# Feature products of an LSH-masked attention: all 64 rows of a head's block instead of 13

## The chip, the cores and the metric

The kernel runs on one core of one Trainium2 chip. Its metric is the device time of one execution in microseconds (us). A core has TensorE (PE; its weight loads are listed as PEld), VectorE (DVE), ScalarE (ACT), GpSimd (POOL), SyncE (SP, which here issues DMAs) and DMA engines. Each engine runs its own list of instructions in order and waits for the others through semaphores. All matmuls write PSUM, which has 128 partitions and 8 banks of 512 float32 values per partition.

## The reference

Four batches of eight heads, 768 positions, 64 values a head. The attention looks only at keys in the same hash bucket as the query; the bucket is the sign pattern of six projections. A gMLP follows.

```
q_bits = (einsum('bhsd,dk->bhsk', q, proj) > 0);  k_bits likewise
mask   = q_bucket[:, :, :, None] == k_bucket[:, :, None, :]      # bucket = the 6 bits as a number
scores = where(mask, q @ k^T / sqrt(64), -1e9)
scores = scores - max(scores);  attn = exp(scores)
attn   = attn / (sum(attn) + 1e-9)
x      = (attn @ v), heads side by side                          # 4 x 768 x 512
...
h = gelu(x @ w_in);  u, v = halves of h;  v_n = layernorm(v) * g_ln
out = x + (u * (w_sg @ v_n + b_sg)) @ w_out
```

## The kernel before, in words

Attention works on 16 head pairs (4 batches, 4 pairs of heads). The two heads of a pair lie one above the other on the 128 partitions: head j has partitions 64j to 64j+63. Every score matmul is issued twice, once a head, with 64 or fewer rows starting at partition 0 or 64, and each writes its own PSUM bank.

For each pair `load` fetches q, k and v; `parts` transposes q and k and splits them into a high and a low half (`hq`, `lq`, `hk`, `lk`: two float32r numbers that together carry the float32 value); `features` (L496, L499) projects them with `pwh`/`pwl` and turns the signs into feature tiles `fq` and `fk`. A feature tile has 128 partitions, in two blocks of 64, one a head (`BL` = 64). In a block row 0 is for the shift of the softmax, rows 1 to 12 hold two signs for each of the six bits, and rows 13 to 63 are zero, because the projection matrix has zero columns there and the threshold and factor of those rows are zero. The product of a query's and a key's feature columns is 0 where all bits agree and at most -2^33 where one differs, so that adding it to the score is the mask.

`largest` (called maxima below) takes a tile of 128 queries. For each half of the keys (384) it adds two products in one bank a head: features first, then `hq` with `hk` (L517). A DVE reduction over each bank (L524) gives the largest score. `shift` turns three tiles' maxima into row 0 of the query features (L533, L539, L545). `weigh` then computes, for half of the queries (384) and tiles of 128 keys, the transposed scores: `hk` with `hq`, `lk` with `hq`, `hk` with `lq`, and the features last, which now also subtract the largest score (L562); ACT takes the exponential into `p` (L568); one call does two key tiles and ends with the product with `v` (L574, eight matmuls with float32 operands); POOL and DVE add up the rows (L583). `finish` divides (L599 to L621) and stores x to DRAM.

The order on each engine is not that of the source. Every step is entered with `plan.add`, with an engine, an estimated cost, a priority, and what it reads and writes. `Plan.order` makes a list schedule out of these and `run` issues the instructions in that order. A maxima group of one key half is entered with a PE cost of 0.36 us, a weigh group of one key tile with 0.71, the value products of two key tiles with 1.48; a cost of 0.09 is added where a group's form differs from that of the group ahead ("row" for maxima and weigh, "col" for value products). Maxima run five query tiles ahead of their use (`AHEAD`). Score tiles take any of seven PSUM banks that is free (`ps_tile`), the value product has the eighth. The splitting of the gMLP's input weights (L352 to L361, mostly DVE) is spread over the first pairs. After attention the pools are released and the gMLP runs, batch by batch (L766, L795, L813, L839).

The change touches `block`, which gives the 13 rows of a head's block, `largest` and `weigh`.

## Time and profile before

| what | us |
|---|---|
| median of 3 runs | 949.92 (948.51 to 952.18) |
| profiled execution, its own time | 944.45 |
| its span, first to last instruction | 942.7 |
| TensorE busy | 916.1 |
| VectorE busy | 620.5 |
| ScalarE busy | 419.5 |
| GpSimd busy | 316.7 |
| granted TensorE clock, mean over the span | 0.971 of full speed |

Attention lasts until about 592 us, the gMLP from there to the end. In a group of the profile, "13*128 13x384" means a matmul with 13 rows (the contraction) and 128 columns that streams 384 elements; x384 is the count of instructions; then come busy time in us, the mean duration of one in ns, and the idle time of the engine ahead of them with what ended it. In the timeline a row gives start and duration in us, and joins neighbours of one kind. A matmul's end is modelled, and neighbours overlap, so the distance of two starts says what a step costs, not the duration.

### The profile page before, as it was taken

How to read it: one execution, taken by the hardware profiler on the slowest of the kernel's cores; microseconds unless marked ns; L12 is line 12 of the kernel's file. 1: busy time of each engine (PE TensorE's matmuls, PEld its weight loads, DVE VectorE, ACT ScalarE, POOL GpSimd, SP SyncE). 2: the span in 40 equal slices, each digit the busy share in tenths (PEclk: the TensorE clock that was granted, in tenths of full speed). 3: DMA queues.
4: the chain of work that ended last, by engine and by line, in shares of the span. 5: the costliest groups of instructions: out<-in, count | busy, mean ns of one | idle time of the engine just before them, and what ended most of it. 6: DMA issues, size and time to landing. Idle time of an engine off the chain costs nothing.

```text
span 942.7 us, 15438 instructions
## 1 busy us (share of the span) xinstructions
PE 916.1 (97%) x5480; PEld 615.7 (65%) x5480; DVE 620.5 (66%) x1369; ACT 419.5 (45%) x926; POOL 316.7 (34%) x342
## 2 busy tenths in 40 slices
PE   7999999999999999999999999887989999999998
PEld 5655555554555555555555555576978998998996
DVE  7777787887778765665565653598996425732930
ACT  2445545544555445454444447355243414522511
POOL 0334444443434344244242426513420320340120
PEclk8999999998999999999998999998999999999999
DMA  5121331331321221221202102342002322103003
GB/s 128 40 79 38 81 87 40 87 88 40 88 65 53 77 51 44 73 55 44 68 27 67 43 19 77 96 153 90 29 23 79 107 85 77 34 17 119 1 1 112
DMA packets 100589, 60.85 MB, mean 65 GB/s; under 512 B 65696, under 2 KB 92320, under 8 KB 100512
## 3 DMA queue, kind: packets, MB, share of 16 engines
q1 hardware_dynamic: 99200, 56.85, 21.2%
q10 hardware_dynamic: 1312, 3.02, 1.0%
q8 instruction: 43, 0.70, 0.3%
q14 instruction: 34, 0.28, 0.1%
HBM read 47.06 MB, written 12.68 MB: 63 GB/s over the span
## 4 chain that ended last, share of the span: by engine, by line
PE 83%; DVE 9%; DMA 4%; issue 1%; SPq 1%; ACT 1%; POOL 0%; ACTq 0%; DVEq 0%
PE g L562 21%; PE av L574 15%; PE g L517 14%; PE ps_vs L813 8%; PE ps_o L839 7%; PE ps_h L795 5%; PE ps_h L766 4%; PE g L496 3%; PE g L474 3%; PE g L539 2%; PE g L599 1%; DMA rs<-r 1%; PE ps_o L844 1%; DMA q<-in_q_dram 1%; DVE owx L353 1%
## 5 line engine op out<-in xcount | busy, mean ns | idle before, releaser
L524 DVE TENSOR_REDUCE mx<-g 128x1 f32<-128x384 f32 x384 | 192.0, 548 | 132.4 <-PE g L517 132.2
L568 ACT ACTIVATE p<-g 128x384 f32<-128x384 f32 x384 | 168.1, 487 | 221.4 <-PE g L562 217.6
L583 POOL TENSOR_TENSOR sum<-sum,p 128x384 f32<-128x384 f32 x128 | 126.9, 1017 | 193.8 <-ACT p L568 180.8
L574 PE MATMUL av<-p,v 128*64 128x385 f32 x768 | 154.9, 527 | 0.0
L517 PE MATMUL g<-hk,hq 64*128 64x384 f32 x384 | 86.2, 445 | 0.0
L574 PEld LDWEIGHTS av<-p,v 128*64 128x64 f32 x768 | 48.5, 141 | 56.0 <-issue 52.4
L562 PE MATMUL g<-fq,fk 13*128 13x384 f32 x384 | 84.5, 436 | 0.0
L562 PE MATMUL g<-hq,hk 64*128 64x384 f32 x384 | 83.6, 431 | 0.0
L583 DVE TENSOR_TENSOR sum<-sum,p 128x384 f32<-128x384 f32 x128 | 68.8, 561 | 19.8 <-ACT p L568 15.5
L517 PE MATMUL g<-fk,fq 13*128 13x384 f32 x384 | 81.3, 417 | 0.0
L562 PEld LDWEIGHTS g<-hq,hk 64*128 64x128 f32 x384 | 36.7, 187 | 64.7 <-issue 49.4
L583 POOL TENSOR_TENSOR sum<-p,p 128x384 f32<-128x384 f32 x64 | 64.0, 1019 | 36.4 <-ACT p L568 35.8
L751 DVE SCALAR_TENSOR_TENSOR h<-h,ps_h 128x384 f32<-128x384 f32 (+1 forms) x56 | 33.2, 605 | 62.8 <-ACT h L750 62.5
L562 PEld LDWEIGHTS g<-fq,fk 13*128 13x128 f32 x384 | 35.4, 181 | 48.6 <-issue 48.6
L562 PE MATMUL g<-hq,lk 64*128 64x384 f32 x384 | 66.1, 339 | 0.0
L562 PE MATMUL g<-lq,hk 64*128 64x384 f32 x384 | 65.6, 336 | 0.0
L839 PE MATMUL ps_o<-woh,gs 128*128 128x512 f32 x192 | 65.5, 402 | 0.0
L813 PE MATMUL ps_vs<-wgh,zh 128*128 128x384 f32 x192 | 64.3, 335 | 0.1
L813 PE MATMUL ps_vs<-wgh,zl 128*128 128x384 f32 x192 | 64.3, 335 | 0.0
L813 PE MATMUL ps_vs<-wgl,zh 128*128 128x384 f32 x192 | 64.2, 334 | 0.0
L517 PEld LDWEIGHTS g<-hk,hq 64*128 64x128 f32 x384 | 36.3, 186 | 39.5 <-issue 39.5
L621 POOL TENSOR_TENSOR xt<-xt,e 128x384 f32<-128x384 f32 x32 | 32.2, 1005 | 83.1 <-ACT e L619 78.4
(127 smaller groups left out, 1679.9 us busy)
## 6 DMA issues: line engine op xcount, KB each, us to landing
q<-in_q_dram SPq DMA_DIRECT2D x32, 192.0 KB, 3.2
k<-in_k_dram SPq DMA_DIRECT2D x32, 192.0 KB, 3.5
v<-in_v_dram SPq DMA_DIRECT2D x16, 384.0 KB, 4.1
rs<-r SPq DMA_DIRECT2D x64, 96.0 KB, 2.9
xs<-xt SPq DMA_DIRECT2D x32, 192.0 KB, 1.8
x<-xs SPq DMA_DIRECT2D x16, 384.0 KB, 3.3
rx<-xs SPq DMA_DIRECT2D x96, 64.0 KB, 2.0
out_dram<-ob SPq DMA_DIRECT2D x24, 256.0 KB, 2.1
```

The source lines that it names most:

```text
L517: nc.tensor.matmul(sc[kh][j]()[:, :SH], x[0]()[r, qs], x[1]()[r, kh * SH:(kh + 1) * SH], start=(n == 0), stop=(n == 1))
L524: plan.add(DVE, 0.56, prio, lambda j=j, kh=kh: nc.vector.tensor_reduce(mx()[:, kh, i, j:j + 1], sc[kh][j]()[:, :SH], axis=AX.X, op=ALU.max ...
L562: nc.tensor.matmul(sc[i][j]()[:, :SH], x()[r, ks], y()[r, cs], start=(n == 0), stop=(n == 3))
L568: plan.add(ACT, 0.5, prio, lambda i=i, j=j: nc.scalar.activation(p[i][j]()[:, :SH], sc[i][j]()[:, :SH], AF.Exp), [sc[i][j]], [p[i][j]])
L574: nc.tensor.matmul(av()[row(j), :SH + 1], st.v()[:, j, kt, :], p[i][j](), start=(kt == 0), stop=(kt == NT - 1))
L583: (nc.gpsimd if e == POOL else nc.vector).tensor_add(sums[j](), first()[:, :SH], p[i][j]()[:, :SH])
L621: plan.add(POOL, 0.98, prio, lambda: nc.gpsimd.tensor_add(xt(), xt(), e()), [xt, e], [xt])
L751: plan.add(DVE, us + 0.07, prio, lambda: nc.vector.scalar_tensor_tensor(h2()[:, :n], h2()[:, :n], 1.0 / GA, ps()[:, :n], op0=ALU.add, op1= ...
L766: nc.tensor.matmul(ps(), x()[:, ts_], w[:, c, FH:FF], start=(c == 0 and n == 0), stop=(c == NC - 1 and n == 2))
L795: nc.tensor.matmul(ps()[:, :SH], w[:, c, fs], x()[:, cs], start=(c == 0 and n == 0), stop=(c == NC - 1 and n == 2))
L813: nc.tensor.matmul(vp(), z()[:, t, fs], w()[:, t, cs], start=(t == 0 and n == 0), stop=(t == NT - 1 and n == 2))
L839: nc.tensor.matmul(po(), a()[:, ts_], w()[:, f, :], start=(f == 0 and n == 0), stop=False)
```

## The change

`block(j)` goes away, and both feature products use `row(j)`, the 64 rows of the head, as the other products of the same groups do. The rows that are added are zero on both sides. No instruction is added or removed, and the costs and dependencies that the planner sees stay as they are.

```
-        def block(b):
-            return slice(b * BL, b * BL + 1 + 2 * NB)
-
         def row(j):
             return slice(j * D, (j + 1) * D)
...
                 for n, x in enumerate((st.ft, st.hi)):
                     for j in range(2):
-                        r = (block, row)[n](j)
-                        nc.tensor.matmul(sc[kh][j]()[:, :SH], x[0]()[r, qs], x[1]()[r, kh * SH:(kh + 1) * SH],
+                        nc.tensor.matmul(sc[kh][j]()[:, :SH], x[0]()[row(j), qs], x[1]()[row(j), kh * SH:(kh + 1) * SH],
                                          start=(n == 0), stop=(n == 1))
...
                 for n, (x, y) in enumerate(((kh, qh), (kl, qh), (kh, ql), (kf, qf))):
                     for j in range(2):
-                        r = block(j) if n == 3 else row(j)
-                        nc.tensor.matmul(sc[i][j]()[:, :SH], x()[r, ks], y()[r, cs], start=(n == 0), stop=(n == 3))
+                        nc.tensor.matmul(sc[i][j]()[:, :SH], x()[row(j), ks], y()[row(j), cs], start=(n == 0), stop=(n == 3))
```

## The prediction, made before the change was run

> **What bounds the kernel now.** I read the page's busy table and its chain by lines first, then busy time by stretches, then TensorE's timeline row by row.

> ```profile
> span 942.7 us, 15438 instructions
> ...
> PE 916.1 (97%) x5480; PEld 615.7 (65%) x5480; DVE 620.5 (66%) x1369; ACT 419.5 (45%) x926; POOL 316.7 (34%) x342
> ...
> PE g L562 21%; PE av L574 15%; PE g L517 14%; PE ps_vs L813 8%; PE ps_o L839 7%; PE ps_h L795 5%; PE ps_h L766 4%; PE g L496 3%; PE g L474 3%; PE g L539 2%; PE g L599 1%; DMA rs<-r 1%; PE ps_o L844 1%; DMA q<-in_q_dram 1%; DVE owx L353 1%
> ```

> PE is busy for 97% of the span, and the two lines that the change touches, L562 and L517, carry 35% of the chain that ended last. The next view gives busy time in stretches that I chose: the start, attention in two parts, the gMLP. Columns: stretch, its length, busy us of PE, PEld, DVE, ACT, POOL with instruction counts, granted PE clock, DMA share, GB/s.

> ```profile
> 0.00:37.00 37.00, 32.02 (x156) 21.60 (x156) 29.43 (x92) 11.04 (x23) 4.23 (x18) 0.86 0.39 100
> 37.00:333.00 296.00, 295.38 (x1950) 160.73 (x1950) 233.91 (x513) 148.76 (x354) 123.58 (x128) 0.98 0.24 66
> 333.00:592.00 259.00, 259.00 (x1698) 138.58 (x1694) 153.56 (x339) 131.44 (x310) 101.73 (x104) 0.97 0.20 53
> 592.00:943.00 351.00, 329.65 (x1688) 294.83 (x1682) 203.64 (x428) 128.29 (x240) 87.20 (x93) 0.97 0.22 68
> ```

> From 37 to 592 us PE never rests. DVE stands at 79% up to 333 us (233.91 of 296) and at 59% after it. So PE sets the pace, with a near second up to 333 us and none behind it. But busy is not streaming, as the starts in the timeline show. A row merges the two heads' matmuls into x2; I call it a couple.

> ```profile
> 380.90 0.44 PE L562 MATMUL g<-fq,fk 13*128 13x384 f32 x2
> 381.18 0.34 PE L517 MATMUL g<-fk,fq 13*128 13x384 f32 x2
> 381.45 0.44 PE L517 MATMUL g<-hk,hq 64*128 64x384 f32 x2
> ...
> 388.98 0.44 PE L562 MATMUL g<-hq,hk 64*128 64x384 f32 x2
> 389.26 0.34 PE L562 MATMUL g<-hq,lk 64*128 64x384 f32 x2
> 389.43 0.34 PE L562 MATMUL g<-lq,hk 64*128 64x384 f32 x2
> 389.70 0.44 PE L562 MATMUL g<-fq,fk 13*128 13x384 f32 x2
> 390.07 0.53 PE L599 MATMUL g<-sum,ones 128*32 128x192 f32 x8
> 390.53 0.44 PE L517 MATMUL g<-fk,fq 13*128 13x384 f32 x2
> 390.90 0.44 PE L517 MATMUL g<-hk,hq 64*128 64x384 f32 x2
> 391.27 0.44 PE L517 MATMUL g<-fk,fq 13*128 13x384 f32 x2
> ```

> From 389.26 to 389.43 a 64-row couple follows a 64-row couple in 0.17 us. Where the row count changes it takes longer: a whole four-couple group from 388.98 to 390.07 takes 1.09 us, with a change of shape at its entry and one before fq,fk, where four steps of 0.174 would take 0.70; a two-couple group from 390.53 to 391.27 takes 0.74 instead of 0.35, again with two changes. Both excesses are 0.39 us, so one change of shape costs 0.195 us: about 0.09 ahead of the first couple of the new shape and 0.10 behind it. It isn't the small row count itself, nor the passage from one line to the other: at 380.90 and 381.18 two 13-row couples of different lines follow each other, and from 380.90 to 381.45 they take 0.55 us, which is two steps of 0.174 and one change.

> **The change part by part.** It alters the rows of two of the operands' slices, nothing else: no instruction, wait, DMA or queue position is added, removed or moved, and since the planner's costs (0.36 and 0.71) and dependencies stay, the written order stays. The feature couples get the shape 64*128 of their neighbours.

> *Stream time of the feature products: nothing.* The 13-row couple at 381.18 has the same 0.34 us as the 64-row couples at 389.26 and 389.43. Both ends of the bound are those rows, and agree.

> *Changes of shape: minus 531 x 0.195 us.* These rows give the counts inside the groups, two matmuls to a couple:

> ```profile
> L562 PE MATMUL g<-fq,fk 13*128 13x384 f32 x384 | 84.5, 436 | 0.0
> ...
> L517 PE MATMUL g<-fk,fq 13*128 13x384 f32 x384 | 81.3, 417 | 0.0
> ...
> L562 PEld LDWEIGHTS g<-lq,hk 64*128 64x128 f32 x384 | 37.2, 189 | 0.0
> ...
> L524 DVE TENSOR_REDUCE mx<-g 128x1 f32<-128x384 f32 x384 | 192.0, 548 | 132.4 <-PE g L517 132.2
> ```

> 192 weigh groups (L562) change shape before their last couple, 192 maxima groups (L517) behind their first: 384. Between groups, the timeline read through has 63 places where a weigh group follows a weigh group (13 to 64 rows) and 84 where a maxima group follows a maxima group (64 to 13). First and last of each:

> ```profile
> 28.83 0.44 PE L562 MATMUL g<-fq,fk 13*128 13x384 f32 x2
> 29.20 0.44 PE L562 MATMUL g<-hq,hk 64*128 64x384 f32 x2
> ...
> 587.82 0.44 PE L562 MATMUL g<-fq,fk 13*128 13x384 f32 x2
> 588.19 0.44 PE L562 MATMUL g<-hq,hk 64*128 64x384 f32 x2
> ...
> 12.84 0.44 PE L517 MATMUL g<-hk,hq 64*128 64x384 f32 x2
> 13.21 0.45 PE L517 MATMUL g<-fk,fq 13*128 13x384 f32 x2
> ...
> 566.88 0.44 PE L517 MATMUL g<-hk,hq 64*128 64x384 f32 x2
> 567.25 0.44 PE L517 MATMUL g<-fk,fq 13*128 13x384 f32 x2
> ```

> Together 531: 29 before 37 us, 271 from there to 333, 231 after. Other changes stay: before and after the value products (128*64), transposes (128*128), sums (128*32). 531 x 0.195 = 103.5 us of PE time: 5.7, 52.8 and 45.0 by stretch.

> *The clock.* Eight stretches of 3.41 us in attention ran at half clock. The rows are the first and the last of them, the stretch before the last, one in which maxima groups run almost alone, and value products at half and at full clock.

> ```profile
> 214.89:218.30 3.41, 3.41 (x14) 1.31 (x10) 2.85 (x7) 0.02 (x1) 0.61 (x1) 0.50 0.11 33
> ...
> 545.98:549.39 3.41, 3.41 (x14) 1.43 (x14) 2.18 (x5) 0.00 (x0) 0.00 (x0) 0.50 0.12 38
> ...
> 542.57:545.98 3.41, 3.41 (x23) 1.98 (x25) 1.99 (x6) 2.55 (x6) 0.00 (x0) 1.00 0.05 6
> ...
> 17.00:27.00 10.00, 10.00 (x35) 6.75 (x35) 9.04 (x21) 1.92 (x4) 0.00 (x0) 0.50 0.03 7
> ...
> 214.64 2.63 PE L574 MATMUL av<-p,v 128*64 128x385 f32 x8
> ...
> 471.80 1.51 PE L574 MATMUL av<-p,v 128*64 128x385 f32 x8
> ```

> Eight value products take 2.63 us in such a stretch, 1.51 otherwise, so one stretch loses 3.41 x (1 - 1.51/2.63) = 1.45 us, and eight lose 11.6: three (4.4) before 333 us, five (7.3) behind. The stretch at 542.57 was busy throughout, but two steps of 0.174 in a maxima group's 0.74 us are 47% streaming, and where such groups run one after another (from 12 us) the clock falls to 0.50 too. So I read the cause as sparse streaming, and without the changes of shape a PE that doesn't wait streams densely: I take the 11.6 us as gained, with nothing as the other end. [...]

> *What is late next.* With PE faster, DVE's reductions (548 ns each, now idle 132.2 us for want of L517) free the score banks on which the next couples wait. Up to 333 us PE alone would need 296 - 52.8 - 4.4 = 238.8 us, and DVE has 233.91 us of work there: 98%. DVE can't be that full while it waits on other engines in turn. The row nearest to a full DVE is in the gMLP:

> ```profile
> 640.00:700.00 60.00, 52.55 (x264) 47.34 (x262) 54.75 (x130) 22.54 (x48) 21.80 (x26) 0.94 0.16 51
> ```

> That is 91%, with DVE in the lead. At 92% the stretch takes 254 us, a gain of 42 instead of 57. Bounds: 238.8 (PE alone) and 266 (88%). Behind 333 us PE would need 259 - 45.0 - 7.3 = 206.7 us and DVE has 153.56, 74% of it; but a tile's four reductions (2.2 us) outlast its two maxima groups (now 1.48 us, then 0.70), so some bursts must wait for banks. I charge 5 us, between 0 and 15 (7%, about the share charged before 333 us), near the low end because value products and weigh groups lie between most tiles: a gain of 47. The start has little to give: DVE was busy 9.04 of 10 us there (row 17.00), so of 5.7 us I take 2 (0 to 5.7). ACT at 131.44 and POOL at 101.73 us fit under 207 easily. The gMLP is untouched and follows whenever attention ends.

> **Sum.** 942.7 us of span lie within 944.45 us of the profiled execution. 944.45 - 2 - 42 - 47 = 853.4. The median of the runs, 949.92, lies 5.5 above the profiled execution; I carry that over: 859.

> **The rivals.** *PE stays the bound throughout.* All 103.5 and 11.6 us come back: 944.45 - 115.1 + 5.5 = 835, and with the start held by DVE 838. For: DVE's 132 us of idling stood almost wholly before reductions that waited for PE. Against: 98% is needed. *DVE bites harder*: 88% up to 333 us (+12), 15 us behind it (+10) and DVE instructions stretched by closer company of POOL's, 2% of its 234 us (+5): 886. For: seven score banks are a short buffer.

> *The weight loads come out.* The load of a 64-row couple takes 189 ns (PEld row), longer than the step of 0.174. If it could not run under a 64-row couple before it, the 384 feature couples would each pay 0.19: 73 us back on PE, 37 and 32 of them in the two attention stretches, which would then take 276 and 239 us; 944.45 - 20 - 20 - 1 + 5.5 = 909. Against: the lq,hk couple at 389.43 had just such a load and came 0.17 us after its neighbour. [...]

> *The clock is lost, and the kernel slower.* If PE, waiting for DVE's reductions, streams so sparsely that the clock stays at half as it does at 17 us, each stretch of 3.41 us loses 1.45. All 74 stretches of the 254 us would cost 107: 859 + 107 = 966. It decides from 66 stretches (96 us, which takes 859 past 950 by 0.5%). For: the start does it. Against: maxima groups run alone only there; later value products of 1.51 us stand between, and 238.8 of the 254 us would be PE work without changes of shape between weigh and maxima groups.

> *Nothing comes back*, because the 0.195 us belongs to the feature tiles, not their row count: 950. Against: 13 rows after 13 rows, at 381.18.

> **How the numbers follow.** Forecast 859 (my own stretch 848 to 872): 0.62. PE bound throughout: 0.15. DVE harder: 0.13. Weight loads: 0.03. Clock lost: 0.02. Nothing: 0.03. Others: 0.02. The range takes the first three: 838 to 886. About 0.5% (4.7 us) is what a measurement of this kernel can tell from no change; faster by more holds all but the clock and the nothing cases, with the others split: 0.94; same 0.03; slower 0.03.

> **What would show it.** Right: the feature groups appear as 64*128 with a mean near 340 ns; 0.17 us steps through whole weigh and maxima groups; attention ends near 500 us; DVE near 92% up to there in its first half; hardly a half-clock stretch in mid-attention; PE rows with idle time ended by L524. Wrong: steps of 0.37 that stay; PEld on the path; PEclk well under 0.97 through attention; or a DVE that idles as before while PE waits for something else, which would put the late step with ACT, the DMAs or the value product's one bank.

## The result and the profile after

The changed kernel takes 866.3 us (median of 4 runs, 864.87 to 868.87) against 950.13 (median of 4, 948.51 to 952.18): a ratio of 0.912, 95% interval 0.909 to 0.915. The forecast was 859, with a range of 838 to 886. The profiled execution took 867.57 us, its span is 865.8.

First the changed kernel's page: span, busy time, and the chain that ended last by engine and by line. L557 is the former L562 (weigh), L513 the former L517 (maxima), L520 the reduction, L569 the value product.

```profile
span 865.8 us, 15438 instructions
...
PE 817.3 (94%) x5480; PEld 616.4 (71%) x5480; DVE 637.3 (74%) x1369; ACT 413.1 (48%) x926; POOL 321.4 (37%) x342
...
PE 61%; DVE 19%; DMA 9%; SPq 4%; ACT 3%; issue 3%; POOL 1%; DVEq 0%; ACTq 0%
```

The count of instructions is the same, and PE's busy time fell by 99 us (916.1 to 817.3) where the execution fell by 77: PE's chain was thinned, and DVE, DMAs and SP's queue stand on more of it than before.

TensorE's timeline after, a weigh group, the spread of the shift, and two maxima groups (start and duration in us):

```profile
391.66 0.44 PE L557 MATMUL g<-hq,hk 64*128 64x384 f32 x2
391.94 0.34 PE L557 MATMUL g<-hq,lk 64*128 64x384 f32 x2
392.12 0.34 PE L557 MATMUL g<-lq,hk 64*128 64x384 f32 x2
392.29 0.33 PE L557 MATMUL g<-fq,fk 64*128 64x384 f32 x2
392.56 0.55 PE L535 MATMUL g<-identr,m 128*128 128x128 f32 x3
393.04 0.44 PE L513 MATMUL g<-fk,fq 64*128 64x384 f32 x2
393.32 0.34 PE L513 MATMUL g<-hk,hq 64*128 64x384 f32 x2
393.49 0.34 PE L513 MATMUL g<-fk,fq 64*128 64x384 f32 x2
393.67 0.34 PE L513 MATMUL g<-hk,hq 64*128 64x384 f32 x2
```

The feature couple at 392.29 follows its neighbour by 0.17 us where 0.27 stood, and the maxima couples at 393.32, 393.49 and 393.67 stand 0.17 apart where 0.37 stood. Only the first couple of a stretch of one shape still shows 0.44. Counted along the whole timeline, the changes of shape fell from 893 to 362, so by exactly 531.

TensorE's order of issue is the same in both kernels, so a given matmul can be sought in both traces. The matmuls that began at 37.36, 333.16 and 590.01 us now begin at 34.08, 295.43 and 508.87. Busy time between these places, before and after (columns as before: PE, PEld, DVE, ACT, POOL, PE clock, DMA):

```profile
37.36:333.16 295.80, 295.18 (x1948) 160.55 (x1946) 233.71 (x513) 148.92 (x355) 123.58 (x128) 0.98 0.24 67
333.16:590.01 256.85, 256.85 (x1682) 137.57 (x1680) 151.41 (x336) 129.82 (x306) 101.23 (x103) 0.97 0.19 53
```

```profile
34.08:295.43 261.35, 246.59 (x1949) 161.47 (x1947) 246.39 (x512) 146.41 (x355) 127.69 (x128) 1.00 0.27 75
...
295.43:508.87 213.44, 210.38 (x1681) 136.95 (x1678) 157.32 (x336) 124.37 (x302) 99.78 (x102) 1.00 0.23 63
...
25.53:517.00 491.47, 470.13 (x3721) 306.87 (x3719) 414.99 (x871) 279.11 (x676) 236.70 (x239) 1.00 0.26 69
```

The start gave 3.3 us, the first part of attention 34.5, the second 43.4. That is 81 us at the last weigh groups; the end of the execution has 77 of them, so 4 are lost in the passage to the gMLP and in the gMLP itself. DVE is busy for 94% of the first part (246.39 of 261.35) and 74% of the second. The last row says that TensorE kept its full clock from 25.5 to 517 us: of the eight stretches at half clock in attention none is left in this execution.

In the first part TensorE was idle for 14.8 us of the 261.35 (246.59 busy). Its waits there, with what ended them (us in total, times, longest):

```profile
PE g L535 <- DVE m L529: 4.9, 6, 0.8
PE g L471 <- DVE mx L520: 4.2, 6, 0.7
PE g L557 <- ACT p L563: 2.0, 5, 0.7
PE g L557 <- DVE mx L520: 1.5, 2, 0.9
PE g L513 <- DVE mx L520: 1.4, 2, 0.8
```

DVE ended 12.0 us of them: 7.1 by reductions that freed a score bank, 4.9 by the small operation on the maxima (L529) ahead of the spread.

The wait at the passage, before and after:

```profile
595.11 0.52 PE L599 MATMUL g<-sum,ones 128*32 128x192 f32 x4 [1.48 <-POOL sum L583]
```

```profile
516.08 0.52 PE L594 MATMUL g<-sum,ones 128*32 128x192 f32 x4 [3.11 <-POOL sum L578]
```

### The profile page after: what moved, and what is told of

Same layout as the page of the kernel before. It is cut to its first block, busy times and chain, and to the rows that moved or that the text cites. A ratio compares the mean times of both kernels' runs of the same rounds, so it can differ in the third digit from the quotient of the medians.

```text
span 865.8 us, 15438 instructions
## 1 busy us (share of the span) xinstructions
PE 817.3 (94%) x5480; PEld 616.4 (71%) x5480; DVE 637.3 (74%) x1369; ACT 413.1 (48%) x926; POOL 321.4 (37%) x342
## 4 chain that ended last, share of the span: by engine, by line
PE 61%; DVE 19%; DMA 9%; SPq 4%; ACT 3%; issue 3%; POOL 1%; DVEq 0%; ACTq 0%
PE g L557 11%; PE av L569 10%; PE ps_vs L808 8%; PE ps_o L834 8%; PE ps_h L790 7%; PE g L513 6%; DVE mx L520 4%; PE ps_h L761 4%; PE g L493 2%; SPq L602 2%; DVE sum L578 2%; DMA rs<-r 2%; DMA sq<-sm 2%; PE g L471 2%; ACT p L563 1%
## 5 line engine op out<-in xcount | busy, mean ns | idle before, releaser
L563 ACT ACTIVATE p<-g 128x384 f32<-128x384 f32 x384 | 162.2, 493 | 133.1 <-PE g L557 126.4
L520 DVE TENSOR_REDUCE mx<-g 128x1 f32<-128x384 f32 x384 | 191.1, 548 | 34.6 <-PE g L513 33.6
L578 POOL TENSOR_TENSOR sum<-sum,p 128x384 f32<-128x384 f32 x128 | 130.3, 1042 | 130.4 <-ACT p L563 86.5
L569 PE MATMUL av<-p,v 128*64 128x385 f32 x768 | 145.6, 500 | 0.0
L557 PE MATMUL g<-hq,hk 64*128 64x384 f32 x384 | 85.5, 395 | 4.5 <-ACT p L563 2.8
L569 PEld LDWEIGHTS av<-p,v 128*64 128x64 f32 x768 | 47.0, 136 | 58.0 <-issue 47.5
L513 PE MATMUL g<-fk,fq 64*128 64x384 f32 x384 | 82.7, 384 | 3.9 <-DVE mx L520 3.7
L557 PEld LDWEIGHTS g<-hq,hk 64*128 64x128 f32 x384 | 42.9, 183 | 58.8 <-issue 35.4
L578 DVE TENSOR_TENSOR sum<-sum,p 128x384 f32<-128x384 f32 x128 | 74.1, 603 | 12.6 <-ACT p L563 9.8
L578 POOL TENSOR_TENSOR sum<-p,p 128x384 f32<-128x384 f32 x64 | 64.5, 1029 | 29.9 <-ACT p L563 28.9
L513 PE MATMUL g<-hk,hq 64*128 64x384 f32 x384 | 73.3, 344 | 0.0
L557 PE MATMUL g<-hq,lk 64*128 64x384 f32 x384 | 73.1, 338 | 0.0
L557 PE MATMUL g<-fq,fk 64*128 64x384 f32 x384 | 71.7, 333 | 0.0
L557 PE MATMUL g<-lq,hk 64*128 64x384 f32 x384 | 71.6, 334 | 0.0
L513 PEld LDWEIGHTS g<-fk,fq 64*128 64x128 f32 x384 | 43.8, 185 | 20.9 <-DVE mx L520 9.8
L771 POOL TENSOR_TENSOR mv<-mv,epsr 128x1 f32<-128x1 f32 x24 | 13.9, 581 | 117.9 <-DVE mv L770 114.9
## 6 DMA issues: line engine op xcount, KB each, us to landing
q<-in_q_dram SPq DMA_DIRECT2D x32, 192.0 KB, 3.3
k<-in_k_dram SPq DMA_DIRECT2D x32, 192.0 KB, 3.5
xs<-xt SPq DMA_DIRECT2D x32, 192.0 KB, 1.8
```

Of the source, the lines that this page charges most:

```text
L513: nc.tensor.matmul(sc[kh][j]()[:, :SH], x[0]()[row(j), qs], x[1]()[row(j), kh * SH:(kh + 1) * SH], start=(n == 0), stop=(n == 1))
L520: plan.add(DVE, 0.56, prio, lambda j=j, kh=kh: nc.vector.tensor_reduce(mx()[:, kh, i, j:j + 1], sc[kh][j]()[:, :SH], axis=AX.X, op=ALU.max ...
L557: nc.tensor.matmul(sc[i][j]()[:, :SH], x()[row(j), ks], y()[row(j), cs], start=(n == 0), stop=(n == 3))
L563: plan.add(ACT, 0.5, prio, lambda i=i, j=j: nc.scalar.activation(p[i][j]()[:, :SH], sc[i][j]()[:, :SH], AF.Exp), [sc[i][j]], [p[i][j]])
L569: nc.tensor.matmul(av()[row(j), :SH + 1], st.v()[:, j, kt, :], p[i][j](), start=(kt == 0), stop=(kt == NT - 1))
L578: (nc.gpsimd if e == POOL else nc.vector).tensor_add(sums[j](), first()[:, :SH], p[i][j]()[:, :SH])
```

## The experiments

Theory A is the prediction's: 0.195 us is paid wherever the array's row shape changes between neighbours, and what the change cannot collect is held back by DVE's load. Rivals B, C and D put the price elsewhere, E and H the rest of the waits; the runs with 32 rows are about the clock. Where no interval is given, a time is that of one execution.

**33 rows.** In the kernel before, the feature slices take 33 rows.

```
-            return slice(b * BL, b * BL + 1 + 2 * NB)
+            return slice(b * BL, b * BL + 33)
```

> Feature couples take 33 of a block's 64 rows. Theory A (the array works in row classes of 32, 64 and 128, and 0.195 us is paid only when the class changes): 33 rows fall in the class of 64, so the time is that of the change, 866 (861 to 871), with steps of 0.17 us around the features. Rival B (any difference of row count between neighbours is paid for): 950, with steps of 0.37 us. Rival C (the time goes with the rows that are used): in between, near 915.

864.69 us, against 952.11 for before in the same series. The steps:

```profile
387.85 0.34 PE L562 MATMUL g<-lq,hk 64*128 64x384 f32 x2
388.02 0.34 PE L562 MATMUL g<-fq,fk 33*128 33x384 f32 x2
388.20 0.33 PE L517 MATMUL g<-fk,fq 33*128 33x384 f32 x2
388.37 0.34 PE L517 MATMUL g<-hk,hq 64*128 64x384 f32 x2
```

33 rows between 64 rows cost nothing: the steps are 0.17 to 0.18 us, where 13 rows had 0.27 and 0.37. Rivals B and C are out. What is paid for is not a different row count but, as theory A has it, a different class.

**32 rows.** The same line with 32.

> Feature couples take 32 rows. Theory A: 32 rows are in the class of 13, all 531 changes stay, 950 (946 to 954). Rival B: 950 too. Rival C: near 915. Together with 33 rows this places the step between 32 and 33, or not.

934.52 us: no theory had that. The steps are those of before (feature couples still 0.37 us from their neighbours), so 32 rows lie in the class of 13 and the class ends between 32 and 33. But 17.6 us are gone all the same. The trace differs from before in the clock, so the kernel was run again, six times:

> The 32-row kernel again, in rounds, because its one look was 15 to 17 us faster than before with the same 0.37 us steps: only the half-clock stretches inside attention were fewer, one where before had eight. [...]

932.15 us (6 runs, 930.86 to 935.59) against 949.51; ratio 0.983, interval 0.979 to 0.986. The gain lasts. The steps of this run and its attention as a whole, then that of before:

```profile
388.26 0.34 PE L562 MATMUL g<-lq,hk 64*128 64x384 f32 x2
388.53 0.44 PE L562 MATMUL g<-fq,fk 32*128 32x384 f32 x2
388.89 0.44 PE L562 MATMUL g<-hq,hk 64*128 64x384 f32 x2
...
30.00:580.00 550.00, 549.13 (x3665) 298.30 (x3663) 392.55 (x861) 281.48 (x667) 226.72 (x232) 0.99 0.23 61
```

```profile
30.00:590.00 560.00, 559.38 (x3673) 302.02 (x3675) 390.28 (x859) 282.64 (x670) 227.35 (x234) 0.98 0.22 60
```

The steps are 0.27 and 0.36 us as before; the half-clock stretches in attention are two (one in the first run) instead of eight. Two stretches against eight are 6 x 1.45 = 8.7 us, close to what the two profiled spans differ by (942.7 to 933.8). The medians differ by 17, since the profiled execution of before (944.45) lies under its median (949.5 here, 950.1 in the first series). The granted clock over the span was 0.983 to 0.987 in the six executions and 0.957 to 0.974 in the eleven of before, so this is not chance. With 32 rows the clock was higher than with 13 at the same steps; why, these runs don't show.

**Mirrored order, 13 rows.** Every second group issues its products in reverse, so that feature couples become neighbours; no row is added.

```
-                for n, x in enumerate((st.ft, st.hi)):
+                for n, (x, rows) in enumerate(((st.ft, block), (st.hi, row))[::-1 if kh == 0 else 1]):
...
-                        r = (block, row)[n](j)
+                        r = rows(j)
...
-                for n, (x, y) in enumerate(((kh, qh), (kl, qh), (kh, ql), (kf, qf))):
+                for n, (x, y) in enumerate(((kh, qh), (kl, qh), (kh, ql), (kf, qf))[::-1 if i == 1 else 1]):
...
-                        r = block(j) if n == 3 else row(j)
+                        r = block(j) if x is kf else row(j)
```

> 13 rows as before, but the products of every second group stand in reverse order, so that feature couples become neighbours: in maxima the first key half adds score then features and the second features then score; in weigh the second key tile begins with its features. By the order of before the changes of shape fall from 893 to 746. Theory A: 147 x 0.195 = 28.7 us less, and perhaps half of the 11.6 us at half clock: 917 (910 to 923). Rival D (the price belongs to the feature couples, or to 13 rows as such, whoever their neighbours are): 950 as before.

910.6 us, at the lower edge of theory A; rival D is out. Two 13-row couples run on (x4 in 0.62 us), and one half-clock stretch is left in attention instead of eight, where the expectation had counted on about half of their 11.6 us.

```profile
387.87 0.34 PE L517 MATMUL g<-hk,hq 64*128 64x384 f32 x2
388.14 0.62 PE L517 MATMUL g<-fk,fq 13*128 13x384 f32 x4
388.69 0.45 PE L517 MATMUL g<-hk,hq 64*128 64x384 f32 x2
```

**64 rows in the maxima alone.**

```
-                        r = (block, row)[n](j)
+                        r = row(j)
```

> Only the maxima groups take 64 rows for their features; weigh keeps 13. Changes of shape fall from 893 to 664: 229 x 0.195 = 44.7 us. Theory A: 944.45 - 44.7, less up to 8 us of half clock and plus up to 6 us that DVE keeps: 902 on the scale of the profiled execution (895 to 908). Where a maxima group follows a weigh group there must be a new step with a change that was not there before. Rival D (half of the feature couples, so half of the gain of 84): 908.

897.03 us, within theory A's interval. The new step is there: 0.36 us from a 13-row weigh couple to a 64-row maxima couple, where before two 13-row couples stood 0.28 apart.

```profile
387.64 0.44 PE L562 MATMUL g<-fq,fk 13*128 13x384 f32 x2
388.00 0.44 PE L517 MATMUL g<-fk,fq 64*128 64x384 f32 x2
388.29 0.34 PE L517 MATMUL g<-hk,hq 64*128 64x384 f32 x2
```

**Halved reductions, with the change and without.** Each maxima reduction reads 192 of 384 scores.

```
-                        mx()[:, kh, i, j:j + 1], sc[kh][j]()[:, :SH], axis=AX.X, op=ALU.max, negate=True),
+                        mx()[:, kh, i, j:j + 1], sc[kh][j]()[:, :SH // 2], axis=AX.X, op=ALU.max, negate=True),
```

> The kernel before, with the same halved reductions (half of the scores is left out of the maximum). If PE alone sets the pace of before: 948 (944 to 951), no gain beyond 0.5%. If DVE already held PE up in the first part: 935 or less.

Before: 947.47 us in one execution, where the kernel before took 939.65 to 953.44 in six executions of the same series: no gain. DVE did not hold PE up there.

> The change, with each maxima reduction reading 192 of its 384 scores (the other half is left out of the maximum), which takes about 0.2 us from each of 384 DVE reductions, some 75 us of DVE's work. Theory A with DVE as the next bound: the stretch that took 261 us falls to what PE alone needs, 239, and the second part loses a few us more: 840 (834 to 846). Rival E (what was left of the gain went to the few score banks, or to ACT and POOL, whatever DVE has to do): 860 or more.

With the change: 855.14 us, between the two theories. The two parts of attention, by the same matmuls:

```profile
29.75:283.44 253.69, 246.87 (x1949) 161.89 (x1947) 206.51 (x512) 145.97 (x355) 124.34 (x128) 1.00 0.28 78
283.44:498.89 215.45, 211.63 (x1682) 137.22 (x1680) 135.62 (x335) 124.63 (x302) 100.13 (x102) 1.00 0.23 62
```

DVE lost 40 us of work in the first part (246.39 to 206.51) and the part became 7.7 us shorter; in the second it lost 22 and the part became 2 us longer. The start gave 4.3 us more (34.08 to 29.75). DVE's reductions matter, but not as a full DVE would.

**Sums where they are planned.** The additions of the third key tile are planned for POOL, but the loop variable's last value puts them on DVE. Here they go to POOL.

```
-                    def add(j=j, i=i, first=p[0][j] if kt == 1 else sums[j]):
+                    def add(j=j, i=i, e=e, first=p[0][j] if kt == 1 else sums[j]):
```

> The change, with the engine of each row-sum addition bound where it is planned: the third key tile's additions go to POOL, as the planner's list has it, instead of to DVE, where the loop variable's last value puts them. That takes 64 additions of 0.6 us, 38 us, from DVE, some 19 us of them in the first 261 us, and gives POOL 64 of 1.04 us. Theory A with DVE as the next bound: DVE's 246 us there become 227, at the same 94% the stretch takes 242 instead of 261; the end of attention may wait 2 us longer for POOL: 850 (842 to 858), faster than the change. Rival E: 862 to 870, or slower by POOL's longer queue.

874.95 us (872.47 to 878.16; ratio to before 0.928, 0.919 to 0.937): slower than the change, and the expectation failed. DVE hardly got lighter: of 66 such additions in the first part 34 are left, but 244.56 us of work remained.

```profile
34.30:302.33 268.03, 253.17 (x1949) 165.34 (x1947) 244.56 (x481) 146.93 (x355) 159.49 (x160) 0.97 0.27 73
```

The part took 6.7 us longer than with the change, and the clock differs: 0.97, with five stretches of 3.41 us at half clock, where the change had none. At 1.45 us each they are worth 7.3 us, while TensorE was idle for as long as with the change (14.9 us; 14.8). Why the half clock came back is not shown.

What became of DVE's gain can be seen on the small operation on the maxima, in the whole run, after and in this kernel:

```profile
L529 DVE SCALAR_TENSOR_TENSOR m<-mx 128x6 fp32r<-128x6 f32 x32 | 12.6, 394 | 1.1
```

```profile
L529 DVE SCALAR_TENSOR_TENSOR m<-mx 128x6 fp32r<-128x6 f32 x32 | 19.1, 597 | 1.1
```

On average it took 204 ns before, 394 with the change and 597 here. But these are mixtures: most of these operations take 170 ns, and those that meet an operation of POOL that began some 0.1 us ahead take up to 0.93 us (with the change). They end with it, as here with the change, where POOL's second addition ends at 203.08 us and DVE's operation at 203.11:

```profile
201.12 1.96 POOL L578 TENSOR_TENSOR sum<-p,p 128x384 f32<-128x384 f32 x2
202.18 0.93 DVE L529 SCALAR_TENSOR_TENSOR m<-mx 128x6 fp32r<-128x6 f32 x1
```

Two of 32 were held up in this way before, 10 with the change, 18 here. TensorE waits for just this operation ahead of the spread (L535): 4.9 us with the change, 10.8 here, while its waits for the reductions in the first part fell from 7.1 us to 4.1.

**The weight splitting spread out.** Each block's load waits for one head pair's features.

```
-        plan.add("SP", 0.55, prio - 2, load, [], [w], dma=0.73 * CW / 256)
+        plan.add("SP", 0.55, prio - 2, load, after, [w], dma=0.73 * CW / 256)
...
+            weight_job(plan, w_tile, *wjobs[n], WSTEP * n + WP, after=[(st.ft[1], 1)])
...
-        for i, job in enumerate(wjobs):
-            weight_job(plan, w_tile, *job, WSTEP * i + WP)
```

> The change, with the splitting of one block of the gMLP's input weights tied to each of the 16 head pairs (its load waits for that pair's features), where it now all lies in the first 300 us of attention. Theory A with DVE as the next bound of the first part only: some 30 us of DVE work move from the first part into the second, which has room; DVE's 246 us there become about 215 and the first part falls from 261 to about 250, while the second grows by 3 at most: 858 (852 to 863). Rival E (the waits belong to the score banks and to POOL's company): 864 or more.

863.05 us (858.15 to 865.98), ratio to before 0.909 (0.904 to 0.913), not to be told from the change's 0.912. And the parts:

```profile
33.25:293.61 260.36, 249.79 (x1948) 162.86 (x1946) 219.54 (x470) 141.62 (x349) 119.48 (x121) 0.99 0.27 70
293.61:509.68 216.07, 211.34 (x1681) 137.50 (x1678) 177.24 (x382) 126.57 (x310) 107.42 (x109) 1.00 0.26 69
```

DVE fell from 94% to 84% of the first part, and the part kept its length (261.35 to 260.36). Alone this would speak against the second half of theory A. But the next kernel issues the same instructions in the same order on every engine up to 500 us, and there the first part took 253.24 us, not far from the 250 that theory A had:

```profile
33.72:286.96 253.24, 246.04 (x1948) 161.48 (x1946) 218.04 (x468) 140.73 (x348) 119.36 (x121) 1.00 0.27 71
```

So one and the same part took 260 us once and 253 once. Of the 7 us, 4.7 arose at one place. First the execution with 260 us, then the same instructions in the other:

```profile
262.15 0.56 DVE L615 TENSOR_TENSOR xt<-un,rs 128x384 f32<-128x384 f32 x1 [2.04 <-DMA rs<-r]
262.96 1.94 DVE L520 TENSOR_REDUCE mx<-g 128x1 f32<-128x384 f32 x4
263.57 0.69 PE L557 MATMUL g<-hq,hk 64*128 64x384 f32 x1 [2.73 <-DVE mx L520]
...
262.92:269.74 6.82, 6.17 (x29) 3.14 (x31) 4.23 (x9) 2.83 (x8) 2.92 (x3) 0.50 0.09 29
```

```profile
258.28 0.56 DVE L615 TENSOR_TENSOR xt<-un,rs 128x384 f32<-128x384 f32 x1
259.70 0.44 PE L557 MATMUL g<-hq,hk 64*128 64x384 f32 x1 [0.84 <-DVE mx L520]
```

In the first, a transfer of the division in `finish` (L607, issued at 254.89 us) took 3.6 us to land, in the other 1.4. DVE stood for 2.04 us ahead of L615, which needs what follows from it, the reductions behind L615 came late, and TensorE waited 2.73 us for them instead of 0.84; from 262.92 to 269.74 us the clock was at half (0.50). The four executions' times spread likewise: 858.15 and 860.29 us at a granted clock of 0.986, 865.81 and 865.98 (the profiled one) at 0.978 and 0.980. So a lighter DVE can give 8 us in the first part, and this run does not refute theory A there.

**Last sums on DVE.** Besides the spreading, the last half pair's row sums go to DVE alone.

```
-                e = ADDS[kt - 1]
+                e = "DVE" if st.n == NPAIR - 1 and hf == 1 else ADDS[kt - 1]
...
-                    def add(j=j, i=i, first=p[0][j] if kt == 1 else sums[j]):
-                        (nc.gpsimd if e == POOL else nc.vector).tensor_add(sums[j](), first()[:, :SH], p[i][j]()[:, :SH])
+                    def add(j=j, i=i, last=st.n == NPAIR - 1 and hf == 1, first=p[0][j] if kt == 1 else sums[j]):
+                        (nc.gpsimd if e == POOL and not last else nc.vector).tensor_add(sums[j](), first()[:, :SH], p[i][j]()[:, :SH])
```

> The same, and the row sums of the last half head pair are added on DVE alone instead of on POOL and DVE, since TensorE waited 3.1 us for POOL's sum at the end of attention and the gain shrank by 4 us there. If that wait is POOL's queue: 3 us less than with the spreading alone. If it is the chain from the last exponential, which stays: no difference beyond 1 us.

875.28 us (871.67 to 878.83), 12 more than with the spreading alone. Both expectations failed. The wait ahead of the last sums became 4.4 us, now for DVE, instead of 3.1 for POOL. By the same matmuls this kernel was 83 us ahead of before at the last weigh groups, 79 behind that wait and 69 at the end; with the spreading alone it was 80, 78 and 78. So most of the loss lies in the gMLP, whose steps the plan had put in another order. What makes it so large was not tried.

**Six score banks.**

```
-        ps_slots = {i: 0.0 for i in range(8 - NAV)}
+        ps_slots = {i: 0.0 for i in range(8 - NAV - 1)}
```

> The change with six PSUM banks for the scores instead of seven (the planner orders the steps for six). Rival E (banks are what the rest of the waits comes from): waits of TensorE for banks grow beyond 60 us in attention, 885 or more. If DVE's load alone makes the waits: 866 to 872.

882.33 us, nearer to rival E. The two parts became 268.86 and 219.47 us, together 13.5 longer; 13 more changes of shape in the new order are 2.5 of these, and two half-clock stretches in the first part, at 1.45 us each, 2.9. TensorE was idle for 14.4 and 2.1 us in the two parts, no longer than with the change (14.8 and 3.1). The remaining 8 us show that banks, or the order made for six of them, bear on the time, though less than E had.

**Maxima groups apart.** Weigh and maxima groups alternate, so that only two banks at a time wait for reductions.

```
-                plan.add(PE, 0.36, prio + 0.01 * kh, lambda kh=kh: mm(kh),
+                plan.add(PE, 0.36, prio + (-0.7, -0.1)[kh], lambda kh=kh: mm(kh),
...
-                    plan.add(DVE, 0.56, prio, lambda j=j, kh=kh: nc.vector.tensor_reduce(
+                    plan.add(DVE, 0.56, prio + (-0.7, -0.1)[kh], lambda j=j, kh=kh: nc.vector.tensor_reduce(
...
-                plan.add(PE, 0.71, prio + 0.01 * i, lambda i=i: mm(i),
+                plan.add(PE, 0.71, prio + 0.6 * i, lambda i=i: mm(i),
```

> The change, with the priorities set so that TensorE's order within a step becomes weigh, maxima, weigh, maxima, value product, where two maxima groups now come in a row. No work is added. Seen so far: relieving DVE by 27 us in the first part (the spread weight splitting) left its length at 260 us, and a shorter single reduction did more; so Theory H: what is left of the waits comes from bursts, four score banks filled within 0.7 us and emptied by four reductions in 2.2 us, and not from DVE's total. Then with two banks at a time the 29.8 and 9.8 us of waits in the two parts of attention fall to less than half: 846 (838 to 853). Theory A as it stood (DVE's total bounds the first part): 862 to 868, the first part stays at 260 us. If the value products now wait for the later exponentials: slower than 868.

861.39 us (859.16 to 864.30), ratio to before 0.908 (0.904 to 0.912): the interval reaches that of the change. Of some 5 us, 14 fewer changes of shape (348) make 2.7. TensorE was idle for 13.4 and 3.6 us in the two parts (14.8 and 3.1 with the change), far from half. Theory H fails as well: the bursts are not what is left.

## Why the prediction was right, and where it was not

*Changes of shape: right, in price and in number.* All 531 went (893 to 362). The experiments confirm each piece: neighbours decide (mirrored order), a change of the maxima alone adds a step where the prediction's reading has one, and a 13-row couple between 64-row couples pays while a 33-row couple doesn't. The stream time is the same, as forecast: 0.34 us for a couple of 13 rows (381.18) and of 64, 0.33 to 0.34 for 33; feature matmuls of 32 rows took 437 and 415 ns on average in the two lines, those of 13 rows 436 and 417.

*The clock: right for the profiled execution, too small for the median, the cause not shown.* The eight half-clock stretches went, and 32 rows bear their price out: six stretches fewer, 8.9 us. But they are not gone for good: the 33-row kernel, with the same steps as the change, had two of them in its first part. That sparse streaming is the cause was the author's reading. The mirrored order, with 147 changes of shape fewer and no row added, left one stretch of eight, which fits it; 32 rows left two, where the streaming was as sparse as before, so it is not the whole cause. The step "I carry that over", 5.5 us from the profiled execution to the median, failed: the other executions of before were slower than the profiled one, the changed kernel's are not (867.57 profiled, 866.3 median). This error hid 7 us of the next ones; that the forecast came so near is in part luck.

*What is late next: the right engine, a term mis-sized, and a proportion that doesn't hold.* The forecast was a gain of 42 us in the first part and 47 in the second; measured 34.5 and 43.4. DVE did become the next bound of the first part: it ended 12.0 of TensorE's 14.8 idle us there. The step that failed is the sum's 233.91 us of DVE work, carried over unchanged. The same instructions took 246.39 us, 5% more (a rival had 2%), with DVE 94% full instead of 92%. The reductions stayed as they were; the row sums on DVE, for one, took 74.1 us in the whole run where they had taken 68.8 (L583, now L578). With the change, 26 of these 128 additions overlapped an operation of POOL and took 818 ns on average, the others 548; before, 13 overlapped one. So "94% busy" holds time in which DVE was held up itself.

Nor does the time follow DVE's work in proportion, as the forecast's 254 = 233.91 / 0.92 supposes: 40 us less work (halved reductions) and 28 us less (spreading) brought the part to 253.7 and 253.2 us, and the latter to 260.4 in another execution. One bank fewer cost some 8 us (six score banks, 882.33), breaking up the bursts gave little (861.39).

With the change some 23 us of waiting in the first part (261.35 less the 238.6 that PE needs alone for these 295.80 us of before) and 9 in the second (213.44 less 204.6) remain, of which the profile shows 14.8 and 3.1 as idle time; the cause of the whole stays open. What holds back a lighter DVE is in part the DMA chain of the division: DVE's list is in order, its operation L615 waits for that chain, and reductions stand behind it, as at 262 us above. In the whole run, with the change and with halved reductions:

```profile
DVE xt L615 <- DMA rs<-r: 18.1, 12, 5.7
```

```profile
DVE xt L615 <- DMA rs<-r: 37.8, 27, 5.6
```

Of these, the first part has 1.4 us with the change and 13.8 with halved reductions. So the chain does not explain what was left of the first part with the change itself, where DVE hardly waited for it; it may be what comes next when DVE is relieved. No run tested this. The chain that ended last has more of DMA and SP's queue after the change (9% and 4%); the page of before had less of both:

```profile
PE 83%; DVE 9%; DMA 4%; issue 1%; SPq 1%; ACT 1%; POOL 0%; ACTq 0%; DVEq 0%
```

*The gMLP "follows whenever attention ends": wrong by 4 us.* At the end of attention POOL's sums ran behind PE, and the faster PE waited longer for them (3.11 instead of 1.48 us); the rest of the 4 us is spread over the gMLP.

*The rivals.* The weight loads stayed hidden: that rival would have made 909, but with loads of 184 and 185 ns on average in the two lines the feature couples at 392.29 and 393.49 come 0.17 us after their neighbours. The lost clock didn't come: 1.00 throughout attention in the profiled execution. Of the two cases beside the forecast, the one in which DVE bites harder lay nearer to the time, and its third term, DVE instructions stretched by POOL's company, is the one that came, larger than it had it.

## What to carry to other kernels

Read the distance between starts on TensorE, not its busy share: a PE that was busy for 100% streamed for about half of the time in some groups (0.35 of 0.74 us), because small matmuls of another row class stood between others. Where operands are padded with zeros anyway, give neighbouring matmuls the same row class (here 13 and 32 rows were in one, 33 and 64 in another), or put those of one class side by side; check on the timeline that the steps fall to the streaming time. And when the pacing engine is relieved, read from a run what ends its waits, not from the next engine's busy share, which can itself hold time of being held up (here 26 of 128 additions took 818 ns instead of 548). Profile a second execution before you call a theory refuted: the same instructions took 260 us once and 253 once here.
